# A fetch moved and a normalisation merged: PReLU slopes after the woven stage, one multiply per head

## The chip, the cores and the metric

The kernel runs on one core of a Trainium2 chip. The metric is the device time of one execution in microseconds (us); lower is better. The kernel before has a median of 765.77 us over three runs (764.23 to 768.6). Engine names in the rows: PE is the matrix engine and PEld its weight loads, DVE is VectorE, ACT is ScalarE, POOL is GpSimd, SP (SPq) is the engine whose queue issues every DMA here.

## The reference

Three layers follow one another, all in fp32.

1. Attention over q, k, v of shape (4 batches, 8 heads, 576 positions, 64). Heads 0 to 3 see a causal window of 32 positions, heads 4 to 7 see the earlier positions that are congruent modulo 32. The scores are scaled by 1/8, masked, put through a softmax, and multiplied by v:

```
attn = np.exp(scores - max);  attn = attn / (np.sum(attn, axis=-1, keepdims=True) + 1e-09)
attn_out = np.matmul(attn, v)
```

2. A maxout layer: h = max(x@w1, x@w2, x@w3) with 512 inputs and 768 features, then h@w_out back to 512.
3. A PReLU layer: h = x@w_in with 2048 features, g = max(h,0) + alpha*min(h,0), with one slope alpha per feature, then g@w_out.

The softmax division is what the second edit touches; alpha is the 2048 slopes that the first one touches.

## The kernel before, in words

**Stages.** A first, *woven* stage handles attention of all four batches, the maxout layer of the first three batches, and the conversion of the weights (loaded as doubles) into pairs of fp32r tiles. A second stage runs the maxout layer of the last batch (`first_net`) while it prepares the PReLU layer's input. A third stage runs the PReLU layer with Strassen-like products. In the trace the woven stage lasts until about 318 us and the third begins near 394 us.

**How attention is tiled.** Each batch has eight units `(cc, hf)`: `cc` picks a pair of heads, `hf` one half of the positions. A unit has two heads (`j` = 0, 1), each with `n` tiles: three of 96x128 for the window heads, and three of 108x108 or two of 126x126 for the strided heads. For one unit the work is: `scores` on PE (line 314), `masked` on DVE (line 322, reads the scores from PSUM, adds the mask, gives the negated maximum), `exponential` on ACT (line 329, gives the row sums), `reciprocal` on DVE (lines 340 and 341), then for each head `normalise` (lines 260 or 262: each tile of `e` times its row reciprocals `rc`), `transposes` on PE (line 355), `keep` (a copy out of PSUM, line 247), and for both heads `values` on PE (line 380) and the high and low parts of x (lines 247 and 250). The normalising of one head is one task with `n` instructions. Maxout products on PE are on lines 542 (gates) and 564 (second matrix).

**What sets the order.** The woven stage's order is not written out. Each piece of work is added to a planner (`Weave`) as a task with the engines it may run on, a cost in ns on each, a position, and what it needs and gives. The planner is a greedy list scheduler: it keeps a clock for each engine, lets a task run on the engine on which it would end first, and among the tasks that could start within 120 ns of the first takes the one with the lowest position. The result is a fixed order of instructions for each engine. Each engine then works through its own list in order, and waits on semaphores. A changed cost of a task can therefore change which engine gets it, and the order of everything behind it. The cost of a VectorE task is commonly `dve(n)`, and the normalising had a formula of its own:

```
def dve(n, ops=1):
    return ("DVE", ops * (75 + 21 * n // 20))
add((("DVE", n * (75 + nk // 2)), ("ACT", n * (140 + 5 * nk // 6))), normalise, pos, ...)
```

By these formulas a head on VectorE counts 417 ns (3 tiles of 128 columns), 387 ns (3 of 108) or 276 ns (2 of 126), and 738, 690 or 490 ns on ScalarE.

**The slopes.** `alpha_sb` is a tile of 128 x 16 fp32 that stays for the whole program. Its DMA (line 729) is SP's first, ahead of the woven stage's first q, k and v (lines 284, 286, 291). It is read once, by a small VectorE instruction (line 786) that makes `nalpha` at the start of the third stage. Behind the woven stage SP issues the first weights of the PReLU layer (`load_h`, line 712) and the rows of its input (`load_x2`, line 669), which VectorE sums and splits (lines 677, 206) between its maxima of the last batch's maxout layer (line 553).

Of the kernel before, what the change touches and what calls it, by code (L numbers as in the profile page):

```python
# [13 lines left out]
AF = mybir.ActivationFunctionType  # L14
ALU = mybir.AluOpType
# [29 lines left out]
class Weave:  # L45
# [16 lines left out]
    def add(self, engines, emit, pos, needs=(), gives=(), makes=(), uses=(), mode=None, slack=0):  # L62
        t = len(self.tasks)
        if engines[0][0] != "PE" and any(key in self.banks for key in uses):
            pos -= self.URGENT
        self.banks.update(key for ring, key in makes if ring == "bank")
        self.tasks.append((engines, emit, pos, needs, makes, mode, slack))
        for ring, key in makes:
            if ring in self.order:
                self.order[ring].append(key)  # L70
        for e in gives:
            self.givers.setdefault(e, []).append(t)
        for key in [key for _, key in makes] + list(uses):
            self.users.setdefault(key, []).append(t)
# [83 lines left out]
def attention_maxout_prelu_kernel(  # L158
# [13 lines left out]
    nc = tc.nc  # L172
# [8 lines left out]
    alpha_sb = const.tile([P, NF2], F32, name="alpha_sb")  # L181

    def build_constants():
        g = nc.gpsimd
        make_identity(nc, ident)
        for m in (mask_l0, mask_l):
            g.memset(m, 0.0)
            g.affine_select(out=m, in_=m, compare_op=ALU.is_ge, fill=BIG, base=32,
                            pattern=[[-1, KT]], channel_multiplier=1)
            g.affine_select(out=m, in_=m, compare_op=ALU.is_ge, fill=BIG, base=-1,  # L190
                            pattern=[[1, KT]], channel_multiplier=-1)
        g.affine_select(out=mask_l0, in_=mask_l0, compare_op=ALU.is_ge, fill=BIG, base=-32,
                        pattern=[[1, KT]], channel_multiplier=0)
        g.memset(mask_s, 0.0)
        ms = mask_s.rearrange("p (r a) -> p r a", a=NA)
        g.affine_select(out=ms, in_=ms, compare_op=ALU.is_ge, fill=BIG, base=0,
                        pattern=[[-NA, 7], [-1, NA]], channel_multiplier=1)
        g.affine_select(out=ms, in_=ms, compare_op=ALU.is_ge, fill=BIG, base=NA - 1,
                        pattern=[[NA, 7], [0, NA]], channel_multiplier=-1)
# [12 lines left out]
    def pool(stack, name, bufs, side="left"):  # L212
        return stack.enter_context(tc.tile_pool(name=name, bufs=bufs, side=side, reuse_waits="tile"))
# [24 lines left out]
    def bank():  # L238
        return ps.tile([P, 512], F32, tag="bank", name="bank")
# [4 lines left out]
    add, tl = weave.add, {}  # L244

    def copy(e, out_, in_):
        (nc.scalar.copy if e == "ACT" else nc.vector.tensor_copy)(out_, in_)  # L247
# [4 lines left out]
    def act(n, chip=False):  # L252
        return ("ACT", (50 if chip else 100) + 5 * n // 6)

    def dve(n, ops=1):
        return ("DVE", ops * (75 + 21 * n // 20))

    def scaled(e, x, by):
        if e == "ACT":
            nc.scalar.activation(x, x, AF.Copy, scale=by)  # L260
        else:
            nc.vector.tensor_scalar(out=x, in0=x, scalar1=by, scalar2=None, op0=ALU.mult)

    def load(kb):
        return (("SP", 3 * kb),)


    def geometry(cc, hf):

        if cc < 2:  # L270
            return QT, KT, [(QT * t, QT * t, t, mask_l0 if t == 0 else mask_l)
                            for t in range(3 * hf, 3 * hf + 3)]
        gs = range(0, 3) if hf == 0 else range(3, 5)
        n = RG[gs[0]][1] * NA
        return n, n, [(RG[g][0] * NA, RG[g][0] * NA, g, mask_s) for g in gs]
# [20 lines left out]
    def attention_tasks(b, cc, hf, pos, step):  # L296

        u = (b, cc, hf)
        nq, nk, tiles = geometry(cc, hf)
        n = len(tiles)  # L300
        slack = 1500 if b else 0
        ek, qk, vk = ("e", u), ("q", b, cc), ("v", b, cc)
# [41 lines left out]
        for j in range(2):  # L344
            trk, ptk = ("tr", u, j), ("pt", u, j)

            def normalise(engine, j=j):
                for i in range(n):
                    scaled(engine, tl[ek][:nq, j, i, :nk], tl["rc", u][:nq, j, i:i + 1])

            def transposes(_, j=j, trk=trk, ptk=ptk):
                tr = tl[trk] = bank()
                tl[ptk] = ptp.tile([P, 3 * KT], F32, tag="pt", name="pt")
                for i in range(n):
                    nc.tensor.transpose(tr[:nk, nq * i:nq * (i + 1)], tl[ek][:nq, j, i, :nk],  # L355
                                        ident[:nq, :nq])

            def keep(e, trk=trk, ptk=ptk):
                copy(e, tl[ptk][:nk, :n * nq], tl[trk][:nk, :n * nq])

            add((("DVE", n * (75 + nk // 2)), ("ACT", n * (140 + 5 * nk // 6))), normalise, pos, needs=[("rc", u)],
                gives=[("nrm", u, j)], uses=[ek])
            add((("PE", 95 * n),), transposes, pos + step, needs=[("nrm", u, j)], gives=[trk],
                makes=[("bank", trk), ("pt", ptk)], uses=[ek], mode="transposes", slack=slack)
            add((act(n * nq, True), dve(n * nq)), keep, pos + step, needs=[trk], gives=[ptk],
                uses=[trk, ptk])
# [6 lines left out]
        def values(_):  # L373
# [11 lines left out]
            needs=[vk] + [("pt", u, j) for j in range(2)] + ([begun] if cc >= 2 and hf else []),  # L385
# [12 lines left out]
        for h in halves:  # L398
# [3 lines left out]
                needs=[pvk], gives=[hik], uses=[pvk])  # L402
# [323 lines left out]

    homes = [("gate", f, g) for f in range(NF1) for g in range(3)] + [("mix", f) for f in range(NF1)]
    build_constants()
    nc.sync.dma_start(alpha_sb, alpha)
    for b in range(B):  # L730
        first, last = (-32, -8) if b == 0 else ((b - 1) * NUNITS + (16 if b == 1 else 3), b * NUNITS - 3)
        step = (last - first) / (len(ATT_UNITS) + 2)
        for i, (cc, hf) in enumerate(ATT_UNITS):
            if i in (0, 2, 4, 5):
                load_task(b, cc, first + step * i - 8)
            attention_tasks(b, cc, hf, first + step * i, step)
# [10 lines left out]
    ax.close()  # L747


    hw = pool(ctx, "hw", 8, "right")  # L750
    xsp = pool(ctx, "xsp", 2, "right")
    tsp = pool(ctx, "tsp", 3, "right")
# [335 lines left out]
```

## Time and profile before

| what | value |
|---|---|
| median of three runs | 765.77 us (764.23 to 768.6) |
| profiled execution, first to last instruction (span) | 762.9 us |
| the span's distance from that median | 2.9 us |
| PE busy | 741.8 us, 97% |
| VectorE busy | 596.8 us, 78% |
| ScalarE busy | 454.7 us, 60% |
| DMA moved | 199.37 MB, 261 GB/s |

The profile gives the profiled execution's own time as its span; what lies around the span isn't listed for it, and the runs' median is 2.9 us longer. Busy time is not the same as need: the ends of pipelined matmuls are modelled, and a matmul at half the clock counts as busy for twice as long. The granted clock (PEclk) is a share of TensorE's full 2.4 GHz: 0.50 is 1.2 GHz.

### The profile page before, as it was taken

The numbers are of one execution on the slowest core, as the hardware profiler recorded it, in microseconds if no ns is written. First come the engines' busy times: TensorE is split into PE (matmuls) and PEld (weight loads), VectorE is DVE, ScalarE is ACT, GpSimd is POOL, SyncE is SP. The second block draws the span as 40 slices with busy tenths as digits, with TensorE's granted clock in tenths as the row PEclk, the third lists the DMA queues.
The fourth block names the chain that finished last, engine by engine and source line by source line (L and its number), as shares of the span: only waits on it lengthen the run. The fifth ranks groups of instructions, "written<-read, shape, count | busy, mean of one in ns | idle before, by whom it ended". The sixth has DMA issues, their size and how long they took to land.

```text
span 762.9 us, 16093 instructions
## 1 busy us (share of the span) xinstructions
PE 741.8 (97%) x5704; PEld 723.0 (95%) x5704; DVE 596.8 (78%) x1670; ACT 454.7 (60%) x1226; POOL 3.2 (0%) x16
## 2 busy tenths in 40 slices
PE   5899999999999999999999999999999999999997
PEld 4699999999999999999999999999999999999997
DVE  5999999888777987336368988878888877888894
ACT  6988897756665775323246566624666644566561
POOL 1000000000000000000000000000000000000000
PEclk9699999999999999999999999999999999999999
DMA  7387769877878856566938889999888999878361
GB/s 245 130 259 232 240 216 326 271 273 255 300 248 282 270 202 213 171 259 192 362 113 285 273 289 320 386 403 334 291 285 301 354 401 328 273 239 259 121 194 59
DMA packets 85471, 199.37 MB, mean 261 GB/s; under 512 B 10640, under 2 KB 40848, under 8 KB 85392
## 3 DMA queue, kind: packets, MB, share of 16 engines
q1 hardware_dynamic: 85392, 198.35, 75.9%
q8 instruction: 45, 0.74, 0.4%
q14 instruction: 34, 0.28, 0.1%
HBM read 148.51 MB, written 49.81 MB: 260 GB/s over the span
## 4 chain that ended last, share of the span: by engine, by line
PE 77%; DVE 12%; DMA 5%; ACT 2%; issue 2%; SPq 1%; DVEq 0%; ACTq 0%
PE bank L542 27%; PE ph L959 20%; PE po L802 15%; PE bank L564 9%; PE bank L314 3%; PE bank L380 2%; PE bank L355 2%; DVE g L796 2%; DVE c L806 2%; DMA w<-wh 1%; DMA w<-wp 1%; DVE e L322 1%; DMA xs<-x 1%; DMA x<-xd 1%; DVE c L964 1%
## 5 line engine op out<-in xcount | busy, mean ns | idle before, releaser
L542 PE MATMUL bank<-x,w 128*128 128x288 f32 x1728 | 236.5, 297 | 0.3 <-DVE t L553 0.3
L542 PEld LDWEIGHTS bank<-x,w 128*128 128x128 f32 x1728 | 231.1, 189 | 2.1 <-DVE t L553 0.6
L959 PE MATMUL ph<-x,w 128*128 128x384 f32 x1008 | 203.4, 337 | 1.8 <-DVE c L964 1.2
L802 PE MATMUL po<-w,g 128*128 128x256 f32 x1296 | 183.8, 282 | 1.7 <-DVE g L796 0.8
L802 PEld LDWEIGHTS po<-w,g 128*128 128x128 f32 x1296 | 175.4, 189 | 4.2 <-DVE g L796 3.2
L959 PEld LDWEIGHTS ph<-x,w 128*128 128x128 f32 x1008 | 168.3, 188 | 3.0 <-DVE c L964 1.9
L964 DVE TENSOR_TENSOR c<-ph,c 128x384 f32<-128x384 f32 x168 | 91.0, 554 | 32.7 <-PE ph L959 31.8
L795 ACT CAST g<-c 128x384 fp32r<-128x384 f32 x96 | 48.5, 505 | 89.7 <-DVE c L946 53.0
L564 PE MATMUL bank<-h,w 128*128 128x288 f32 x576 | 79.9, 297 | 0.4 <-DVE nm L322 0.4
L564 PEld LDWEIGHTS bank<-h,w 128*128 128x128 f32 x576 | 76.9, 188 | 1.8 <-DVE nm L322 0.8
L250 DVE TENSOR_TENSOR w<-word,w 128x512 fp32r<-128x512 f32 x88 | 55.4, 637 | 23.9 <-ACT w L247 23.5
L329 ACT ACTIVATE e<-e,nm 96x128 f32<-96x128 f32 (+2 forms) x176 | 68.0, 394 | 6.0 <-DVE nm L322 6.0
L916 ACT ACTIVATE c<-c 128x384 f32<-128x384 f32 x96 | 50.5, 526 | 33.9 <-DVE c L964 32.9
L247 ACT CAST w<-word 128x512 fp32r<-128x512 f32 x88 | 50.6, 582 | 32.0 <-DMA wh<-w 17.7
L917 ACT ACTIVATE c<-c,nalpha 128x384 f32<-128x384 f32 x96 | 59.2, 617 | 3.1
L920 DVE SCALAR_TENSOR_TENSOR c<-c 128x384 f32<-128x384 f32 x96 | 53.0, 552 | 9.0 <-ACT c L917 9.0
L796 DVE TENSOR_TENSOR g<-c,g 128x384 fp32r<-128x384 f32 x96 | 52.9, 551 | 1.9 <-ACT g L795 1.9
L796 DVE TENSOR_TENSOR g<-k,g 128x384 fp32r<-128x384 f32 x72 | 36.8, 550 | 14.4 <-ACT g L795 14.4
L439 ACT ACTIVATE word<-raw 128x512 f32<-128x512 f32 x56 | 37.4, 677 | 11.5 <-DMA raw<-in_w 5.9
L445 DVE SCALAR_TENSOR_TENSOR word<-raw,word 128x512 uint32<-128x512 uint32 x56 | 38.8, 693 | 1.9
L631 DVE TENSOR_TENSOR t<-bank,t 128x288 f32<-128x288 f32 x72 | 32.6, 452 | 7.8 <-PE bank L542 7.1
L795 ACT CAST g<-k 128x384 fp32r<-128x384 f32 x72 | 33.4, 515 | 7.8 <-PE po L802 4.4
(72 smaller groups left out, 679.8 us busy)
## 6 DMA issues: line engine op xcount, KB each, us to landing
w<-wh SPq DMA_DIRECT2D x72, 512.0 KB, 5.0
raw<-in_w SPq DMA_DIRECT2D x50, 512.0 KB, 4.5
w<-wo SPq DMA_DIRECT2D x48, 512.0 KB, 5.9
w<-wp SPq DMA_DIRECT2D x36, 512.0 KB, 6.3
wh<-w SPq DMA_DIRECT2D x24, 512.0 KB, 3.7
xd<-xst SPq DMA_DIRECT2D x28, 384.0 KB, 3.5
x<-xd SPq DMA_DIRECT2D x28, 384.0 KB, 8.1
wp<-w SPq DMA_DIRECT2D x24, 256.0 KB, 3.0
```

What stands on the lines that cost most here:

```text
L247: (nc.scalar.copy if e == "ACT" else nc.vector.tensor_copy)(out_, in_)
L250: nc.vector.tensor_tensor(out=out_, in0=x, in1=y, op=ALU.subtract)
L329: nc.scalar.activation(tl[ek][:nq, j, i, :nk], tl[ek][:nq, j, i, :nk], AF.Exp, bias=tl["nm", u][:nq, j, i:i + 1], scale=-1.0, accum_out=tl ...
L542: nc.tensor.matmul(acc, words["gate", f, g][:, wi, cc * P:(cc + 1) * P], xt[b, cc, hf][:, xi, :], start=n == 0, stop=n == 3 * NCC - 1)
L564: nc.tensor.matmul(acc, words["mix", f][:, wi, dc * P:(dc + 1) * P], st["h", hf, f][:, xi, :], start=n == 0, stop=n == 3 * NF1 - 1)
L795: nc.scalar.copy(g[:, 0], x)
L796: return g, lambda: nc.vector.tensor_tensor(out=g[:, 1], in0=x, in1=g[:, 0].bitcast(F32), op=ALU.subtract)
L802: nc.tensor.matmul(bank[:, NH * half:NH * (half + 1)], g[:, gi, t * P:(t + 1) * P], w[:, wi, off:off + NH], start=first and i == 0, stop=l ...
L917: nc.scalar.activation(a, a, AF.Copy, scale=nalpha[:, f:f + 1])
L920: nc.vector.scalar_tensor_tensor(out=a, in0=h, scalar=0.0, in1=a, op0=ALU.max, op1=ALU.add)
L959: nc.tensor.matmul(bank, words["h", n, i][:, wi, off + c * P:off + (c + 1) * P], x2h[blk, k, c][:, xi, :], start=m == 0, stop=m == 5)
L964: nc.vector.tensor_tensor(out=out_, in0=bank, in1=other, op=ALU.add)
```

## The change

The slopes' DMA moves from SP's first place to the place behind the whole woven stage, ahead of `load_h`. A head's `n` tiles are normalised on VectorE by one multiply of two tensors, in which the reciprocals, one per row and tile, are repeated over the columns with a broadcast access pattern; on ScalarE the head stays `n` instructions. The planner's cost of the VectorE form becomes `dve(n * nk)`: 478, 415 and 339 ns for the three kinds of head. The helper `scaled` goes.

```
@@ build of the tasks
-    def scaled(e, x, by):
-        if e == "ACT":
-            nc.scalar.activation(x, x, AF.Copy, scale=by)
-        else:
-            nc.vector.tensor_scalar(out=x, in0=x, scalar1=by, scalar2=None, op0=ALU.mult)
@@ attention_tasks
             def normalise(engine, j=j):
-                for i in range(n):
-                    scaled(engine, tl[ek][:nq, j, i, :nk], tl["rc", u][:nq, j, i:i + 1])
+                e, rc = tl[ek][:nq, j, :n, :nk], tl["rc", u][:nq, j, :n]
+                if engine == "ACT":
+                    for i in range(n):
+                        nc.scalar.activation(e[:, i], e[:, i], AF.Copy, scale=rc[:, i:i + 1])
+                else:
+                    nc.vector.tensor_tensor(out=e, in0=e, in1=rc.unsqueeze(2).to_broadcast([nq, n, nk]),
+                                            op=ALU.mult)
-            add((("DVE", n * (75 + nk // 2)), ("ACT", n * (140 + 5 * nk // 6))), normalise, pos, needs=[("rc", u)],
+            add((dve(n * nk), ("ACT", n * (140 + 5 * nk // 6))), normalise, pos, needs=[("rc", u)],
                 gives=[("nrm", u, j)], uses=[ek])
@@ order of the program
     build_constants()
-    nc.sync.dma_start(alpha_sb, alpha)
     for b in range(B):
...
     conv_x.close()
     ax.close()
+    nc.sync.dma_start(alpha_sb, alpha)
     hw = pool(ctx, "hw", 8, "right")
```

## Rows read from the trace of the kernel before

**Rows 1.** The page's head and its line of TensorE's busy time.
```profile
span 762.9 us, 16093 instructions
PE 741.8 (97%) x5704; PEld 723.0 (95%) x5704; DVE 596.8 (78%) x1670; ACT 454.7 (60%) x1226; POOL 3.2 (0%) x16
```

**Rows 2.** Busy time by stretch: length, each engine (instructions), granted clock, DMA share, GB/s.
```profile
12.00:24.00 12.00, 10.52 (x106) 8.03 (x106) 9.94 (x67) 10.68 (x46) 0.00 (x0) 1.00 0.51 173
24.00:26.00 2.00, 0.25 (x3) 0.06 (x1) 2.00 (x15) 2.00 (x12) 0.00 (x0) 1.00 0.82 241
26.00:40.00 14.00, 12.73 (x89) 10.65 (x90) 12.21 (x59) 11.53 (x46) 0.00 (x0) 0.51 0.45 146
42.00:130.00 88.00, 87.51 (x759) 84.59 (x754) 85.55 (x287) 74.29 (x236) 0.00 (x0) 1.00 0.77 253
130.00:320.00 190.00, 189.56 (x1613) 183.27 (x1612) 145.34 (x489) 122.61 (x391) 0.00 (x0) 1.00 0.75 251
```

**Rows 3.** The chain of waits, 0 to 45 us: start, length, what.
```profile
3.08 5.16 DMA k<-in_kTs
8.37 1.44 PE bank L314 x12
...
20.32 0.83 PE bank L314 x12
...
26.13 0.21 DVE e L262
26.34 0.14 issue
26.47 0.72 PE bank L355 x3
27.20 1.53 PE bank L314 x12
28.72 1.16 PE bank L380 x12
```

**Rows 4.** Waits of PE over the whole span: total us, times, longest.
```profile
PE bank L355 <- DVE e L262: 5.7, 3, 2.2
...
PE bank L542 <- DVE t L553: 0.3, 1, 0.3
```

**Rows 5.** SP's issues in order of time at the start: start, length, line, what.
```profile
0.74 0.39 SPq L729 DMA_DIRECT2D alpha_sb<-in_alpha  x1
1.19 0.42 SPq L284 DMA_DIRECT2D q<-in_qT  x1
```

**Rows 6.** VectorE's normalising before 42 us: count, ns least/median/most, forms.
```profile
L262 DVE TENSOR_SCALAR e<-e,rc x38: 265/276/289, 11.4 to 37.7; 96x128 f32<-96x128 f32 x18, 108x108 f32<-108x108 f32 x12, 126x126 f32<-126x126 f32 x8
```

**Rows 7.** Instructions in order of time, 0 to 30 us, of line 262.
```profile
11.36 1.20 DVE L262 TENSOR_SCALAR e<-e,rc 108x108 f32<-108x108 f32 x6
...
12.89 0.87 DVE L262 TENSOR_SCALAR e<-e,rc 126x126 f32<-126x126 f32 x4
...
22.95 0.67 DVE L262 TENSOR_SCALAR e<-e,rc 96x128 f32<-96x128 f32 x3
```

**Rows 8.** Groups by form: busy us, mean ns, idle before and its releaser.
```profile
L796 DVE TENSOR_TENSOR g<-k,g 128x384 fp32r<-128x384 f32 x72 | 36.8, 550 | 14.4 <-ACT g L795 14.4
...
L443 DVE TENSOR_SCALAR word<-word 128x512 uint32<-128x512 uint32 x56 | 23.4, 418 | 1.1 <-ACT word L439 1.0
...
L250 DVE TENSOR_TENSOR h<-t,h 128x288 fp32r<-128x288 f32 x36 | 16.1, 450 | 2.2 <-ACT h L637 2.2
...
L250 DVE TENSOR_TENSOR w<-word,w 128x256 fp32r<-128x256 f32 x16 | 6.7, 421 | 2.4 <-ACT w L247 2.1
```

**Rows 9.** The chain of waits, 300 to 345 us.
```profile
322.15 5.67 DMA w<-wh
...
327.84 6.63 DMA xs<-x
...
337.30 0.38 DVE t L553
```

**Rows 10.** The only reader of the slopes.
```profile
L786 DVE TENSOR_SCALAR nalpha<-alpha_sb x1: 168/168/168, 394.1 to 394.1; 128x16 f32<-128x16 f32 x1
```

## The prediction

> **What bounds the kernel now.** I read the page's head first: PE is busy for 741.8 of the 762.9 us [rows 1], so at most some 21 us are to be had anywhere without taking matmuls away, and the change takes none. Next the busy time by stretch, to see where those 21 us lie [rows 2]. From 42 to 130 us PE is busy for 87.51 of 88 us, from 130 to 320 us for 189.56 of 190. Nothing that VectorE saves there can show: the two stretches together hold 0.9 us of idle PE, although VectorE itself is at 85.55 of 88 us in the first. The losses sit ahead of 42 us, where the first batch's attention has to be finished before there are maxout products to fill PE with. Two things are to be seen there. PE waits, and in the longest case (24 to 26 us) it is busy for 0.25 of 2 us while VectorE and ScalarE are both full. Then, from 26 to 40 us, the granted clock is 0.51, that is nearly all of it at 1.2 GHz: the same twelve score matmuls that took 0.83 us at 20.32 take 1.53 us at 27.20 [rows 3]. So the stage that the change can move is the first 42 us, and what counts in it is how early PE starts, the gaps, and how long the clock is low.
>
> The waits of PE say who makes the gaps [rows 4]: 5.7 us in three waits of the transposes (line 355) for VectorE's normalising (line 262). That is exactly the instruction that is rewritten. But in the chain of waits each of these gaps shows only a fraction of a microsecond of line 262 itself (0.21 us at 26.13 [rows 3]); ahead of it stand masks and low parts that VectorE's list has in front of it. The normalising is late because of the order, not because it is long.
>
> **The slopes at the start.** Their issue starts at 0.74 us and the first q's at 1.19 [rows 5], so every load of the first batch moves forward by 0.45 us. Those loads are on the chain: the second k lands 5.16 us after 3.08, and scores start at 8.37 [rows 3]; the masks, exponentials and transposes follow from there. If the loads are limited by their issue or by the rate of the DMA engines, the shift arrives whole in both cases. The gain lies between 0 and 0.45 us; I take 0.45.
>
> **The slopes behind the woven stage.** The only reader is at 394.1 us [rows 10], more than 70 us later, so the landing costs nothing. The issue itself is another 0.45 us in SP's queue, now ahead of the weights and x rows of the next stage. These are not quite free: the chain runs through their DMAs (w at 322.15, xs at 327.84, 6.63 us) to VectorE's sums and the maximum at 337.30 [rows 9], for which PE waits 0.3 us [rows 4]. Any delay there adds to a wait that already ends last. Between 0 (the DMA engines are backed up anyway) and 0.45; I take 0.45. The two halves of this edit cancel.
>
> **The merged multiply, its length.** Before 42 us there are 38 single-tile multiplies [rows 6]: 18 of 128 columns (6 heads), 12 of 108 (4 heads), 8 of 126 (4 heads, two tiles each). Three of 128 take 0.67 us, six of 108 take 1.20 and four of 126 take 0.87 [rows 7], so a head costs 0.67, about 0.62 and about 0.44 us. The merged form is not in the trace; the nearest rows are multiplies' siblings, subtractions of two fp32 tensors in SBUF [rows 8]: 550 ns for 384 columns, 450 for 288, 421 for 256. For 324 columns I interpolate 450 + 36 x (550 - 450)/96 = 488 ns, for 252 I take 420. Saved per head: 0.12, 0.13 and 0.02 us; in the first 42 us 6 x 0.12 + 4 x 0.13 + 4 x 0.02 = 1.3 us of VectorE. Bounds: the repeated operand could be read free of charge but no faster than a dense one, so 1.3 us is the upper end of the gain; at the other end, if its pattern is taken at half the pace of the dense rows, a head of 384 columns takes 0.95 us and the 14 heads lose about 3.5 us. I take the dense rows, since they differ only in the second operand's address.
>
> Column by column the single-tile form is the faster: 418 ns for 512 columns against 276 for 128 is 0.37 ns a column [rows 6, 8], the two-tensor form has (550 - 421)/128 = 1.0. The Trainium skill (VectorE: DVE Perf Modes, "The perf-mode tier table") says the same, that an fp32 tensor_scalar in SBUF runs at twice the rate of tensor_tensor, and by that rate alone the edit would lose 0.2 us on each head of 384 columns. The trace decides the other way for tiles this short: three short starts cost more than the slower columns do.
>
> **The merged multiply, who waits.** The transposes of a head could begin when its first tile was done; now they wait for all of it. At the three waits the first tile took 0.2 to 0.3 us and the merged one takes about 0.5, so the transposes begin 0.2 to 0.3 us later; but they then run without being paced by the tiles, and win back 0.1 to 0.2. I charge 0.1 us at each of the three, 0.3 in all; with nothing won back it would be 0.9.
>
> **What the freed VectorE time is worth.** In the old order little: from 27.20 on the chain is PE itself at the low clock, and ahead of 24 us there is slack at VectorE (9.94 of 12 us busy [rows 2]). Between 0 and 1.3 us; I take half, 0.7, since the planner can use it: it now counts 478 ns for a head of 384 columns that takes some 550, where it counted 417 for one that took 670. Its clock runs less ahead of the chip's.
>
> **Sum.** -0.45 + 0.45 + 0.3 - 0.7 = -0.4 us. Against the profiled span that is 762.5; the median of the runs lies 2.9 us above the span, so against it 765.77 - 0.4 = 765.4 us.
>
> **What the sum can't hold.** The planner's costs of VectorE heads rise by 61, 28 and 63 ns, so its whole order may come out differently, and some heads may pass to ScalarE. Behind 42 us PE is full and a new order has little to win and not much to lose. Ahead of it, an order decides whether there is a gap like that at 24 us, and so what the clock does.
>
> **Rivals.**
> *A. The gap at 24 us goes, and the clock stays up.* For it: the gap is made by the order of VectorE's list, and the low clock begins right behind it [rows 2, 3]. The Trainium skill (TensorE: Matmul & The Clock Gate, "What's actually happening") has the throttled state as the default that activity releases; that agrees with this place. Price: 12.73 us of busy PE at the low clock would shrink by 1 - 0.83/1.53 = 46%, or 5.8 us; but VectorE is busy for 12.21 of those 14 us, and if its work stays in the stretch only 1.8 go. Middle 3.8, with the sum 761.6 us, and 759.6 at best. Against it: three waits for the same line show that VectorE's list is crowded anyway, and a gap need only move.
> *B. The new order adds a gap, on the slower side.* One more wait of PE like that at 24 us (2.2 us [rows 4]) at a place before the products have begun in earnest, followed by eight more busy us at the low clock (8 x 0.46 = 3.7): +5.9, with the sum 771.3 us. It decides the sign from about 4 us of such loss on. For it: in-order engines, a wait that now needs a whole head, and a crowded ScalarE (10.68 of 12 us [rows 2]) which gets any heads that leave VectorE. Against it: the planner's costs are nearer to the chip's than before.
> *C. The repeated operand is slow.* The 3.5 us of VectorE from above, of which PE sees perhaps two thirds because VectorE has little slack here: +2.7 with the other terms (without the 0.7), 768.5 us. Nothing in the trace speaks for it.
>
> **How the numbers follow.** Forecast (order much as now) 0.53, its own range 763.5 to 767; A 0.24; B 0.18; C 0.05. About 0.5%, 3.8 us, is what a measurement here tells from no change; the runs shown spread over 4.4. Faster by more than that is most of A (0.18, its better outcomes) and a little of the forecast (0.04): 0.22. Slower is most of B (0.15) and a part of C and of the forecast (0.03): 0.18. The rest, 0.60, is within. The range reaches to A's best, 759.5, and to B, 771.5.
>
> **What would show it.** SP's first issue is q at about 0.74 us, and the first scores start near 4.6 instead of 5.02. Line 262's group becomes some 40 two-tensor multiplies of about 550, 490 and 420 ns; 900 ns would be C. The windows ahead of 42 us tell A from B: the granted clock of 26 to 40 us, and the time from which PE is full. Behind it, PE stays full to 320 us. I would be wrong if PE's idle time grew behind 42 us, or if the start of dense products moved by over 4 us in either direction without a change of the clock.

## The result, and the profile after

The changed kernel takes 770.85 us (median of 12 runs) where the kernel before takes 766.41: a ratio of 1.0059, 95% interval 1.0044 to 1.0075. It is slower by about 4.4 us. The profiled execution has a span of 766.4 us against 762.9 [rows 1]. PE's busy time hardly moved, and VectorE has 74 instructions fewer:

```profile
span 766.4 us, 16024 instructions
PE 740.4 (97%) x5704; PEld 722.1 (94%) x5704; DVE 593.1 (77%) x1596; ACT 454.6 (59%) x1227; POOL 3.2 (0%) x16
```

The same stretches as in [rows 2], with the columns named there, and one more at the end, 320 to 400 us:

```profile
...
24.00:26.00 2.00, 1.63 (x24) 1.24 (x20) 1.45 (x9) 2.00 (x12) 0.00 (x0) 1.00 0.69 187
26.00:40.00 14.00, 10.43 (x108) 8.53 (x109) 12.94 (x73) 13.72 (x60) 0.00 (x0) 0.88 0.59 194
42.00:130.00 88.00, 88.00 (x758) 85.27 (x757) 83.87 (x255) 72.30 (x224) 0.00 (x0) 1.00 0.76 256
130.00:320.00 190.00, 190.00 (x1615) 183.55 (x1614) 143.17 (x458) 122.67 (x391) 0.00 (x0) 1.00 0.72 244
...
320.00:400.00 80.00, 74.05 (x544) 73.82 (x543) 37.90 (x80) 24.46 (x59) 0.00 (x0) 0.96 0.65 234
```

In these two executions the changed kernel is ahead up to 320 us. The clock of 26 to 40 us is 0.88 instead of 0.51, and PE has no idle time at all from 42 to 320 us. Then 6 of 80 us are idle, at a clock of 0.96. PE's waits over the whole span say what it waited for (us in total, times, longest), as in [rows 4]:

```profile
PE bank L541 <- DVE t L552: 5.9, 1, 5.9
...
PE bank L354 <- DVE e L347: 5.6, 3, 3.0
```

The first row is the 0.3 us wait of [rows 4] (lines moved by one), grown to 5.9 us. PE's instructions in order of time place it: the first twelve product units of the second stage, then the wait, the rest, and the start of the third stage. First the kernel before, then the changed kernel:

```profile
318.20 19.20 PE L542 MATMUL bank<-x,w 128*128 128x288 f32 x144
337.72 38.38 PE L542 MATMUL bank<-x,w 128*128 128x288 f32 x288 [0.32 <-DVE t L553]
...
395.82 6.52 PE L959 MATMUL ph<-x,w 128*128 128x384 f32 x36 [0.67 <-ACT xo L651]
```

```profile
315.04 19.20 PE L541 MATMUL bank<-x,w 128*128 128x288 f32 x144
340.18 40.36 PE L541 MATMUL bank<-x,w 128*128 128x288 f32 x288 [5.95 <-DVE t L552]
...
399.42 6.44 PE L958 MATMUL ph<-x,w 128*128 128x384 f32 x36
```

In the kernel before, the second stage began at 318.20 us, so the woven stage of this execution ended 3.16 us *earlier*. The third stage began at 399.42 us instead of 395.82, so the second stage took 84.38 us instead of 77.62, 6.76 longer. From there on both need 367.0 us. The 6.76 are 5.6 us more of that wait, 2.0 us because the next 288 products took 40.36 us where they took 38.38 at the full clock (behind the wait the granted clock was 0.50 from 340 to 344 us), less 0.9 us at the end of this stage, most of it a wait of 0.67 us that only the kernel before has.

**How the wait comes about.** The chain of waits in that place, answering to [rows 9]:

```profile
319.58 2.42 DMA wp<-w
...
323.33 6.34 DMA w<-wh
...
329.69 7.25 DMA xs<-x
...
339.76 0.38 DVE t L552
...
340.18 4.92 PE bank L541 x20
```

Read backwards: PE waits for a maximum (line 552) that stands in VectorE's list behind the sums of the x rows (line 676); the rows land at 336.93 us; they are queued behind eight weight loads (line 711); the first of those waits until 322.00 us for the landing of the last converted weight of the woven stage (`wp<-w`). Its issue shows in SP's list. First the kernel before, then the changed kernel (start, length, line, what):

```profile
311.17 3.70 SPq L575 DMA_DIRECT2D x<-xo  x4
315.31 0.52 SPq L477 DMA_DIRECT2D wo<-w  x1
315.88 1.29 SPq L477 DMA_DIRECT2D wp<-w  x2
317.27 3.40 SPq L575 DMA_DIRECT2D x<-xo  x4
320.76 4.32 SPq L712 DMA_DIRECT2D w<-wh  x8
```

```profile
314.71 3.22 SPq L574 DMA_DIRECT2D x<-xo  x4
318.03 0.52 SPq L476 DMA_DIRECT2D wo<-w  x1
318.60 1.49 SPq L476 DMA_DIRECT2D wp<-w  x2
320.14 0.62 SPq L748 DMA_DIRECT2D alpha_sb<-in_alpha  x1
322.01 4.36 SPq L711 DMA_DIRECT2D w<-wh  x8
```

Before, the last three weight stores stand ahead of the last four stores of x2 and are issued by 317.17 us, 1 us before PE enters the second stage. In the new order they stand behind them and are issued by 320.09, 5 us after PE has entered it. The place behind the x2 stores is not all of it. Those are issued by 317.93 us; the last weight store goes out at 319.58, as soon as its weight is done (319.55). ScalarE had begun that weight late, after a wait for the landing of an earlier weight store. These are the last conversions, the high part on ScalarE and the low part on VectorE, in the kernel before and then in the changed one:

```profile
313.94 0.93 ACT L247 CAST w<-word 128x512 fp32r<-128x512 f32 x2
314.59 1.03 DVE L250 TENSOR_TENSOR w<-word,w 128x512 fp32r<-128x512 f32 x2 [2.66 <-ACT w L247]
```

```profile
318.69 0.41 ACT L247 CAST w<-word 128x256 fp32r<-128x256 f32 x1 [2.53 <-DMA wp<-w]
319.12 0.43 DVE L250 TENSOR_TENSOR w<-word,w 128x256 fp32r<-128x256 f32 x1 [2.25 <-ACT w L247]
```

The last weight is done 2.6 us ahead of PE's entry before, and 4.5 us behind it after. So the new order has the whole tail of the conversions late against PE, not the stores alone. Measured from that entry, the weight loads start at 6.97 us instead of 2.56, and the rows land at 21.9 instead of 16.3. PE can run twelve units ahead, 19.2 us, and then stands still.

### The profile page after: what moved, and what is told of

Read it like the earlier page. It is cut to its first block, busy times and chain, and to the rows that moved or that the text cites. A ratio compares the mean times of both kernels' runs of the same rounds, so it can differ in the third digit from the quotient of the medians.

```text
span 766.4 us, 16024 instructions
## 1 busy us (share of the span) xinstructions
PE 740.4 (97%) x5704; PEld 722.1 (94%) x5704; DVE 593.1 (77%) x1596; ACT 454.6 (59%) x1227; POOL 3.2 (0%) x16
## 4 chain that ended last, share of the span: by engine, by line
PE 82%; DVE 8%; DMA 4%; ACT 4%; issue 2%; SPq 0%; DVEq 0%
PE bank L541 28%; PE ph L958 21%; PE po L801 15%; PE bank L563 10%; PE bank L308 3%; PE bank L379 2%; PE bank L354 2%; DVE g L795 2%; DVE c L805 2%; DMA w<-wh 1%; ACT e L323 1%; DMA xs<-x 1%; DMA x<-xd 1%; DVE c L963 1%; ACT g L794 1%
```

## The experiments

Each run is compared with the kernel before on the same chip. The table reads three numbers from each trace: the start of the second stage, its length up to the first product of the third, and the ratio.

| kernel | second stage begins | lasts | ratio to before (95%) |
|---|---|---|---|
| before | 318.20 | 77.62 | |
| changed | 315.04 | 84.38 | 1.0059 (1.0044 to 1.0075) |
| slopes moved alone | 318.65 | 78.15 | 1.0008 (0.9985 to 1.0030) |
| merged multiply alone, old cost | 317.40 | 77.41 | 0.9974 (0.9950 to 0.9997) |
| new cost alone | 319.68 | 84.27 | 1.0085 (1.0060 to 1.0111) |
| changed, slopes first | 315.25 | 85.81 | 1.0060 (1.0036 to 1.0084) |
| changed, rows first | 320.48 | 76.24 | 0.9961 (0.9939 to 0.9982) |
| before, rows first | 317.45 | 76.86 | 0.9974 (0.9949 to 0.9998) |
| changed, pace 2.4 | 319.19 | 77.25 | 0.9996 (0.9970 to 1.0023) |
| both edits, old cost, rows first | 320.36 | 76.16 | 0.9965 (0.9941 to 0.9989) |
| changed, sums later | 318.76 | 83.33 | 1.0043 (1.0023 to 1.0063) |
| changed, rows first, pace 2.4 | 318.49 | 76.16 | 0.9950 (0.9934 to 0.9967) |
| changed, second trace | 316.68 | 81.83 | one run |

**The change in three parts.** The slopes' fetch alone:

```
     build_constants()
-    nc.sync.dma_start(alpha_sb, alpha)
...
+    nc.sync.dma_start(alpha_sb, alpha)
     hw = pool(ctx, "hw", 8, "right")
```

> The kernel before with only the slopes' fetch moved behind the woven stage; every engine's order but SP's first and one later issue is that of before. My theory (the loss comes from the order that the planner makes of the new cost, at the seam behind the woven stage): first scores 0.4 us earlier, the wait of PE for the maximum at the seam grows from 0.3 to about 0.8 us, total within 1 us of before, 765.5 to 767. Rival (the fetch in its new place delays the weights and the x rows and makes the 5.9 us wait of the changed kernel): a wait of 4 us or more at the seam and 770 us.

Measured 767.1 us, 1.0008, 0.1 us above my range. The second stage's wait went from 0.3 to 1.0 us, and the first scores moved forward by 0.4. The total can't be told from no change: the interval allows from 1.1 us less to 2.3 us more.

The merged multiply, with the planner's cost left as it was (shown against the changed kernel; the slopes' fetch is in front again, which isn't shown):

```
-            add((dve(n * nk), ("ACT", n * (140 + 5 * nk // 6))), normalise, ...
+            add((("DVE", n * (75 + nk // 2)), ("ACT", n * (140 + 5 * nk // 6))), normalise, ...
```

> The merged multiply on VectorE with the planner's old cost and the slopes first, so that the order of tasks is that of before. My theory: nothing is lost at the seam (wait of PE under 1 us there), the total is within 2 us of before, 764.5 to 767.5, what is left being the start, where the clock may fall at another moment. Rival (the merged instruction itself costs time, since transposes wait for a whole head): 769 us or more, with more idle PE ahead of 42 us.

Measured 764.29 us, 0.9974: about 2 us faster than before, if the interval is taken at its middle, and 0.2 to 3.8 by its ends. The merged instruction isn't what costs time; it is a small gain.

The cost alone, with one instruction per tile as before:

```
-            add((("DVE", n * (75 + nk // 2)), ("ACT", n * (140 + 5 * nk // 6))), normalise, ...
+            add((dve(n * nk), ("ACT", n * (140 + 5 * nk // 6))), normalise, ...
```

> The kernel before with only the planner's cost of a VectorE head changed to 478, 415 and 339 ns; the instructions stay one per tile and the slopes first. My theory: it has the changed kernel's order, with the last weight stores behind the last x2 stores in SP's queue, so PE waits 4 to 6.5 us for line 553's maximum at the seam and the clock falls there; total 769.5 to 772. Rival (merged instruction or fetch at fault): no long wait at the seam, 765 to 767.5.

Measured 773.56 us, 1.0085, 1.6 us above my range. This is the whole loss and a little more, with not one instruction of the change in it. Its waits of PE and its SP list show the same seam:

```profile
PE bank L542 <- DVE t L553: 6.5, 1, 6.5
```

```profile
319.74 3.17 SPq L575 DMA_DIRECT2D x<-xo  x4
323.00 0.53 SPq L477 DMA_DIRECT2D wo<-w  x1
323.58 1.64 SPq L477 DMA_DIRECT2D wp<-w  x2
327.18 4.29 SPq L712 DMA_DIRECT2D w<-wh  x8
```

The three parts add up: 0.08 - 0.26 + 0.85 = 0.67%, where the whole change has 0.59 (0.44 to 0.75).

**Is it the fetch in its new place?** The changed kernel with the slopes in front again:

> The changed kernel with the slopes' fetch back in SP's first place. My theory (the fetch hides behind the wait for the last weight store at the seam, so all that it changes is the start): the wait for line 553's maximum stays at 5 to 6.5 us, total 770 to 772. Rival (the fetch delays the weights and rows): the wait falls by 1 us or more and the total to 768 or less.

Measured 770.91 us; the wait was 6.8 us, somewhat above what I expected. The fetch isn't the cause.

**Is it the landing of the rows?** Rows ahead of weights, in the changed kernel and then in the kernel before:

```
+    early = early_x2(1, 2, 1)
+    next(early)
     for n in range(2):
         load_h(n, (0, 2, 1, 3))
-    early = early_x2(1, 2, 1)
...
-        next(early, None)
+        if n:
+            next(early, None)
```

> The changed kernel with the four x row loads issued ahead of the eight weight loads of the PReLU layer instead of behind them. My theory (PE waits at the seam because VectorE's sums, ahead of the maxima in its list, wait for rows that land 22 us into the stage): the rows land at least 8 us earlier, the 5.9 us wait and the low clock behind it go, 770.9 - 5.9 - 2.0 = 763 us, 761.5 to 764.5, faster than before too. Rival (the sums' place in VectorE's list or the clock is at fault, not the landing): the wait stays over 3 us and the total at 768 or more.

> The kernel before with the x row loads ahead of the PReLU weight loads, nothing else. My theory (the seam costs only where the rows land late; before, PE waits 0.3 us there): 765.5 to 766.5, at most 0.5 us faster than before. Rival (issuing the rows first is worth several us in itself, whatever the woven stage's order, so that the run with the rows first said nothing about the seam): 763 us or less.

The changed kernel falls to 763.67 us, 0.9961. The rows land 10.6 us into the stage instead of 21.9, and all 432 gate products run without a break:

```profile
320.48 57.28 PE L541 MATMUL bank<-x,w 128*128 128x288 f32 x432
```

The kernel before comes to 764.09 us, between the two expectations: more than the 0.5 us that I gave it. Its second stage got 0.8 us shorter, that of the changed kernel 8.1; the rest of its gain lies in a woven stage that ended 0.75 us earlier, which is inside the spread told of below.

**Is it the tail of the woven stage?** With a faster pace of the conversions the planner puts the last three weight stores ahead of the last x2 stores again:

```
-    pace = 2.6
+    pace = 2.4
```

> The changed kernel with the weight conversions' pace in the planner at 2.4 instead of 2.6 units: the woven stage is planned anew, and in its order the last three weight stores again stand ahead of the last four x2 stores in SP's queue, as in the kernel before. My theory (those stores' place decides when the PReLU weights and the x rows behind them are issued): the wait of PE at the seam is under 2 us and the total 762 to 767. Rival (the wait comes from the merged multiply or the faster woven stage as such): 4 us or more of wait, 769 or more.

Measured 765.45 us. SP's list and PE's wait:

```profile
316.30 0.53 SPq L476 DMA_DIRECT2D wo<-w  x1
316.87 1.83 SPq L476 DMA_DIRECT2D wp<-w  x2
318.75 2.70 SPq L574 DMA_DIRECT2D x<-xo  x4
321.50 0.43 SPq L748 DMA_DIRECT2D alpha_sb<-in_alpha  x1
322.02 4.35 SPq L711 DMA_DIRECT2D w<-wh  x8
```

```profile
PE bank L541 <- DVE t L552: 0.8, 1, 0.8
```

The wait is 0.8 us with the merged multiply and the new cost both in place. The last weight is done at 318.16 us, 1.0 us ahead of PE's entry into the second stage, and the PReLU weight loads start 2.83 us behind that entry, close to the 2.56 of the kernel before. The whole woven stage is planned anew here, so the run ties the wait to the tail of the order; that the place of the stores alone would do it isn't shown, since no run moved only them.

**Does it reach PE through VectorE's list?** The sums four maxima later, the loads unmoved:

```
-    early = early_x2(1, 2, 1)
+    early = early_x2(1, (6, 2), (1, 0))
```

(The lines that let `early_x2` take a pair of gaps aren't shown.)

> The changed kernel with VectorE's first sums of the x rows placed four maxima later in its list (behind the seventh product unit of the stage instead of the third; the splits of the second half closer together to fit); the loads stay where they are. My theory (the rows' late landing reaches PE only through VectorE's list, where the sums stand ahead of the maxima that free PE's banks): PE can run four more units, 6.4 us, before it waits, so the 5.9 us wait shrinks to under 1 us with the rows landing as late as before; total 762.5 to 765. Rival (PE waits for something else that the late weights hold up, or the time comes back as a later wait): 768 or more.

Measured 769.93 us, 1.0043: half a miss. The rows landed 22 us into the stage as before, and yet PE ran through its 432 gate products, as I expected. But the time came back behind them, as the rival's last clause had it:

```profile
318.76 57.57 PE L541 MATMUL bank<-x,w 128*128 128x288 f32 x432
...
382.49 19.76 PE L563 MATMUL bank<-h,w 128*128 128x288 f32 x129 [4.18 <-ACT h L203]
```

With the same work of splitting the rows squeezed into fewer units, ScalarE's list met stores that had not landed (`xst` on line 203 waited 3.45 us for `xd<-xst` at 374.66), and the last h, behind them, was late. So the place in VectorE's list does pass the late rows on to PE; moving it is no cure.

**Versions that beat both.** Both edits with the old cost and the rows first, and the changed kernel with the rows first and the faster pace:

> Both edits of the change, but with the planner's old cost, so the order of tasks is that of before, and the x rows ahead of the PReLU weights. My theory: the merged multiply's 2 us are kept, the start is 0.4 us earlier and the wait of 1 us at the seam goes: 766.1 - 2.0 - 0.4 - 0.7 = 763.0, 761.5 to 764.5. Rival (the gains do not add, since PE's start depends on where the clock falls): 765 or more.

> The changed kernel with the rows first and the weight conversions' pace at 2.4. My theory (two cures of one wait, so they don't add): no wait at the seam, within 0.3% of the run with the rows first, 762.5 to 765.5. Rival (the faster pace is worth time of its own): 761.5 or less.

They come to 763.89 us (0.9965) and 761.37 us (0.9950). The first is in its range; but its interval (0.9941 to 0.9989) holds the ratio of the merged multiply alone and that of the kernel before with the rows first, both 0.9974, as well as the sum of the two gains, so that they add isn't shown. The last is the fastest kernel here, below my range and just where its rival had it. Its interval overlaps that of the changed kernel with the rows first, so that the pace has a worth of its own isn't shown either.

**The changed kernel again.**

> The changed kernel once more, unedited, for a second trace of it. My theory: the second stage lasts 84 to 86 us again (5.9 to 7 us of wait and the low clock), while the end of the woven stage, 315.0 us in the first trace, moves by up to 5 us as it did in the run with the rows first, which has the same woven order. Rival (the long wait is an accident of the first trace): a second stage under 80 us.

The wait was 4.0 us and the second stage lasted 81.83 us: shorter than I expected, but longer than the rival's 80 and the 77.62 of the kernel before. The tail was less late here: the last weight was done 2.8 us behind PE's entry instead of 4.5, since ScalarE waited 0.78 us ahead of it instead of 2.53.

## Why the prediction was wrong, step by step

- **The step that failed** is the sentence "Behind 42 us PE is full and a new order has little to win and not much to lose." In the sum, a new order behind 42 us stands at nothing. But it also changes the *end* of the woven stage, where PE being full says nothing about when the last converted weight is done and stored. One of my own signs of being wrong, idle time of PE that grows behind 42 us, came true there: a wait of 5.9 us, where it had been 0.3. I had the place in my hands: of the seam I wrote that "Any delay there adds to a wait that already ends last", and then charged it with the 0.45 us of the moved fetch alone. The new cost alone put 84.27 - 77.62 = 6.65 us on the second stage.
- **Rival B had the sign and not the place.** Its gap was to come ahead of 42 us with the low clock behind it. The gap came at 334 to 340 us. Twenty products behind it took 4.92 us, 0.246 each against 0.133 in a full stretch, so the clock's part was there too (2.0 us where B had 3.7). That B's 771.3 us is so close to the measured 770.85 is luck: the sum of a wait and a low clock of about its size, by another cause in another stage.
- **Rival A came true in part in the first trace, but it isn't shown to be the change's doing.** The clock of 26 to 40 us rose from 0.51 to 0.88, and dense products began at 38.62 us instead of 42.35, although a gap of 3.0 us remained (up to 29.66 us). The low clock behind the gap became short (0.66 from 30 to 32 us, 0.50 from 32 to 34, 0.98 from 34 to 36) without the gap going. The Trainium skill (TensorE: Matmul & The Clock Gate, "What's actually happening") has activity release the throttle; by these traces a gap in this stretch doesn't decide how long the low clock lasts. Nor does the order alone: the kernel before with only its rows moved, whose woven stage is unchanged, has 0.88 in the same stretch too (its row is below), and one trace of the new order (sums later) has 0.61.

```profile
26.00:40.00 14.00, 11.42 (x116) 9.08 (x114) 13.26 (x71) 13.09 (x54) 0.00 (x0) 0.88 0.49 165
```

- **The slopes at the start: right for the first scores, not for what follows.** SP's first issue is q at 0.74 us, and the first scores start at 4.62 instead of 5.02. But the scores of the second k, which are on the chain, start at 8.13 instead of 8.37 (8.15 with the slopes moved alone): the shift does not arrive whole. In all the runs with the slopes moved they start between 7.72 and 8.63, so even the 0.2 us that is left lies inside the spread.
- **The slopes behind the woven stage: right in the kernel before's order** (wait 0.3 to 1.0 us), and free in the changed kernel, where SP waits until 322.0 us anyway.
- **The merged multiply, its length: right.** I had 550, 488 and 420 ns; the groups (busy us, mean ns, idle before) show 547, 490 and 413, and the repeated operand costs nothing:

```profile
L347 DVE TENSOR_TENSOR e<-e,rc 96x384 f32<-96x384 f32 x21 | 11.3, 547 | 0.0
L347 DVE TENSOR_TENSOR e<-e,rc 108x324 f32<-108x324 f32 x10 | 4.6, 490 | 0.1
L347 DVE TENSOR_TENSOR e<-e,rc 126x252 f32<-126x252 f32 x11 | 4.3, 413 | 0.1
```

- **What it is worth: the sign was right.** I had 0.3 lost on transposes and 0.7 won; alone it wins 2.0 us. My 0.4 lies inside its interval (0.2 to 3.8), so the size is not told apart.
- **"Its clock runs less ahead of the chip's"** was no argument for the sign. The planner's tasks end with the woven stage, so what the next stage waits for does not count in its order, whatever its costs; and a difference of 28 to 63 ns a head reordered the tail.

## What to carry to other kernels

When a change touches a cost that a scheduler reads, price the order's ends first: what is done last in each engine's and queue's list, when, and what the next stage needs from it. A full engine in the middle of a stage is no cover for its last stores. And split such a change into instruction and cost: here the instruction won about 2 us and the cost lost about 6.5.

## What the runs showed of the hardware that I had not expected

The same order of instructions does not end at the same time. Five traces with the changed kernel's woven order enter the second stage at 315.04, 315.25, 316.68, 318.76 and 320.48 us. In the slowest, PE met waits of 0.6 us around 121 us, and the eighteen products behind them took 4.18 us where the first trace of the changed kernel has 2.63 (the granted clock was 0.50 from 123 to 125 us). It was 1.2 us behind that trace at about 109 us and 4.2 us behind it at about 127. First the changed kernel, then the one with the rows first:

```profile
119.49 2.63 PE L563 MATMUL bank<-h,w 128*128 128x288 f32 x18
```

```profile
120.46 0.47 PE L354 MATMUL bank<-ident,e 96*128 96x96 f32 x3 [0.61 <-DVE t L630]
121.52 0.71 PE L308 MATMUL bank<-k,q 64*126 64x126 f32 x8 [0.59 <-ACT pt L247]
122.16 4.18 PE L563 MATMUL bank<-h,w 128*128 128x288 f32 x18
```

The chain of waits of the slow trace names what came ahead of the two waits, a weight store that landed 6.55 us after its issue and held up ScalarE:

```profile
113.18 6.55 DMA wh<-w
...
119.75 0.41 ACT w L247
...
121.17 0.31 ACT pt L247
```

In the first trace the store in this place was issued at 112.17 us, and ScalarE went on at 116.71, 4.5 us later. By this chain, a landing that took 2 us longer than in another execution became two short waits of PE, and the products behind them lost 1.5 us at the low clock. Why the landing took longer was not tried. How much the woven stage itself gains from the new order is left open for that reason: the traces of the old order enter the second stage at 317.40 to 320.36 us, which overlaps. The second stage's length is not left open: with the loads unmoved it is 77.41 to 78.15 us in the old order, and 81.83 to 85.81 in the new one.
